# Transposing K from rows of 128 columns, and reading it with a step of two in the score matmuls

## The chip, the core and the metric

The kernel runs on one core of one Trainium2 chip. The time is that of the whole launch on that core, in device microseconds; the figure quoted for a kernel is the median of its runs. Inputs and outputs are bfloat16 in the chip's main memory (HBM). The core has a matrix engine (TensorE; PE in the profile, and PEld for its weight loads), three elementwise engines (VectorE, DVE; ScalarE, ACT; GpSimd, POOL), and a queue engine (SyncE, SP) that here only issues transfers. The transfers are carried out by the core's 16 DMA engines.

## The reference

Two attention blocks, A and B, of the same shape, with weights and caches of their own, are computed one after the other, and their results stand side by side in the output.

```
B, Sq, D = 16, 144, 448;  H, Sk, Dh = 16, 512, 256        # for A and for B
q      = (x @ wq), split into H heads                      # [B, H, Sq, Dh]
scores = einsum("bhqd,bhkd->bhqk", q, k_cache) * Dh**-0.5
p      = softmax(scores, axis=-1)
o      = einsum("bhqk,bhkd->bhqd", p, v_cache)
result = (o, heads joined) @ wo                            # [B, Sq, D]
out    = concatenate([result_A, result_B], axis=-1)
```

There are 2 x 16 x 16 = 512 pairs of batch and head. For each of them, K and V are 512 rows of 256 columns. The scores of one pair sum over the 256 columns of a head, which is more than the 128 rows of the matrix engine, so each score matmul is done in two halves of 128 columns that add up in the same accumulator.

## The kernel before

A "unit" is one pair of batch and head; eight units are a supergroup (64 of them), four are a group. The 144 queries of a unit are split into a part A of 112 queries and a part B of 32, so that four units' B parts fill the 128 output rows of the matrix engine. For each unit or group the work is:

- Q (function `t_q`, L314): eight matmuls of 128 rows by 144 columns make the transposed queries; VectorE or ScalarE scales them and copies them to `qt_sb` (L326, L330).
- SB (`t_sb`, L342): once for each supergroup, 16 matmuls make the part B scores of eight units. Four units share one output bank, each in its own 32 columns of the array (`tile_position=(0, 32 * j)`), so four matmuls can be in the array at a time. The stationary operand is 32 queries, the moving operand is a unit's 512 columns of transposed K.
- SA (`t_sa`, L418): for each unit, two matmuls (one for each half of the head) make the part A scores; the stationary operand is 112 queries, the moving operand 512 columns of transposed K.
- Softmax: VectorE takes the maximum (L354, L429), ScalarE the exponential and the row sum (L364, L440), VectorE the reciprocal (L374, L450), GpSimd multiplies (L382, L458).
- TA and TB (L471, L394): the matrix engine transposes the probabilities, 128 columns at a time. The columns are taken with a step of four elements from `pa_sb` and `pb_sb`; here the probabilities are the stationary operand and the identity is the moving one. VectorE copies the result out (L481, L403).
- PV (`t_pv`, L504): eight matmuls with V as the stationary operand; ScalarE copies the result into `ring` (L519).
- OP (`t_op_piece`, L542): the output projection, in pieces of two matmuls of 448 columns that are spread between the other work.

The order of each engine's instructions is written out by the program before the launch: a loop over slots `i` adds the steps of the units at fixed distances from each other (projection 15 slots ahead of PV, part A scores 5 ahead, part B scores 7 ahead), and a recording class works out which semaphores each step must wait for. Nothing is decided at run time; each engine runs its list in order.

K gets to the chip already transposed. `t_load_k` (L284 to L291) issues one transposing transfer for each supergroup on SP's queue: 4096 rows of 256 columns, which are 2 MB. The tile `kt_sb` has `NK` = 3 slots; in each of them lie, for each of the 128 partitions, first the 4096 elements of the head's first half (columns 0 to 127) and then the 4096 of its second half. Partition p holds columns p and 128 + p. V comes by plain transfers of 1 MB for each group (`t_load_v`, L299), also with three slots; x is transposed as K is (L280, L281); wq (L259, L261) and wo (L269) are plain transfers. All of these stand in one list on SP, sorted by the slot at which they are due. A transfer whose slot in SBUF is still being read makes SP wait, and everything behind it waits too.

Of the kernel before, what the change touches and what calls it, by code (L numbers as in the profile page):

```python
# [5 lines left out]
BF16 = mybir.dt.bfloat16  # L6
# [116 lines left out]
def bass_concat_heads__mha_block_cached__gqa_block_cached__near_ridge_kernel(  # L123
# [14 lines left out]
    ks = (A_k_cache, B_k_cache)  # L138
# [5 lines left out]
    H, SK, DH = A_k_cache.shape[1], A_k_cache.shape[2], A_k_cache.shape[3]  # L144
# [18 lines left out]
    NK, NV, NXG = 3, 3, 3  # L163
# [11 lines left out]
    with contextlib.ExitStack() as es:  # L175
        def sb(name, shape, dt):
            return es.enter_context(nc.sbuf_tensor(name, shape, dt))
# [4 lines left out]
        wq_sb = sb("wq_sb", [128, 4, H * DH], BF16)  # L182
        wo_sb = sb("wo_sb", [128, NWO, D], BF16)
        ring = sb("ring", [128, NWO, RC], BF16)
        kt_sb = sb("kt_sb", [128, NK, 2, 8 * SK], BF16)
        v_sb = sb("v_sb", [128, NV, 4, 4 * DH], BF16)
        xt_sb = sb("xt_sb", [128, NXG, 4, XB * SQ], BF16)
        qt_sb = sb("qt_sb", [128, NQT, 2, SQ], BF16)
# [29 lines left out]
        sems = {n: es.enter_context(nc.semaphore("s_" + n)) for n in sem_names}  # L218

        def unit(U):  # L220
            pr, r = divmod(U, NU)
            b, h = divmod(r, H)
            return pr, b, h
# [60 lines left out]
        def t_load_k(SG):  # L284
            pr, r0 = divmod(8 * SG, NU)
            sl = SG % NK
            src = ks[pr].rearrange("b h k d -> (b h k) d")[r0 * SK:(r0 + 8) * SK, :]

            def e(q):
                return q.dma_start_transpose(kt_sb[:, sl, :, :], src).then_inc(sems["kt%d" % sl], 16)  # L290
            S.add(SP, e, writes=[(("kt", sl), SG)], dma_sem="kt%d" % sl, name="k%d" % SG)  # L291

        def t_load_v(G):
# [39 lines left out]
        def t_sb(SG):  # L333
            ksl = SG % NK

            def e(t):
                ins = None
                for dc in range(2):
                    for jj in range(8):
                        U = 8 * SG + jj  # L340
                        j = jj % 4
                        ins = t.matmul(sb_ps[jj // 4][32 * j:32 * j + 32, :], lhsT=qt_sb[:, U % NQT, dc, QA:SQ],  # L342
                                       rhs=kt_sb[:, ksl, dc, jj * SK:(jj + 1) * SK], start=(dc == 0), stop=(dc == 1),
                                       tile_position=(0, 32 * j))
                return ins
            S.add(PE, e, reads=[(("qt", (8 * SG + jj) % NQT), 8 * SG + jj) for jj in range(8)] + [(("kt", ksl), SG)],
                  writes=[(("sbb", 0), ("s", 2 * SG)), (("sbb", 1), ("s", 2 * SG + 1))], banks=["sb0", "sb1"],
                  name="SB%d" % SG)
# [60 lines left out]
        def t_sa(U):  # L409
            SG = U // 8  # L410
            ksl = SG % NK
            bank = U % 2
            ko = (U % 8) * SK

            def e(t):
                ins = None
                for dc in range(2):
                    ins = t.matmul(sa_ps[bank][0:QA, :], lhsT=qt_sb[:, U % NQT, dc, 0:QA],  # L418
                                   rhs=kt_sb[:, ksl, dc, ko:ko + SK], start=(dc == 0), stop=(dc == 1))
                return ins  # L420
            S.add(PE, e, reads=[(("qt", U % NQT), U), (("kt", ksl), SG)], writes=[(("sap", bank), ("s", U))],
                  banks=["sa%d" % bank], name="SA%d" % U)
# [162 lines left out]
        for XG in range(NXGT):  # L585
            pr, j = divmod(XG, Bn // XB)
# [15 lines left out]
        for SG in range(NSG):  # L602
            dl = 8 * SG - LSB
            lo = 8 * (SG - NK) + 7 - LS + 1 if SG >= NK else s_min
            plan(lo, dl, 12, t_load_k, SG)
# [46 lines left out]
        while True:  # L652
# [51 lines left out]
            if 0 <= u < NT:  # L704
                t_pv(u)
                t_evac_ot(u)
                pr, b, h = unit(u)
# [19 lines left out]
            for bank in ("op", "qp"):  # L727
                while fifo[bank] and fifo[bank][0][2] <= i and credit >= 1 and (bank == "qp" or i >= op_hold):
# [3 lines left out]
                    pr = r // NCH  # L732
# [68 lines left out]
```

## Time and profile before

| | before |
|---|---|
| median of 3 runs | 1215.51 us (1214.79 to 1217.66) |
| profiled execution, first to last instruction (its span) | 1210.9 us |
| TensorE busy | 1176.6 us (97% of the span) |
| weight loads (beside the matmuls) | 902.6 us (75%) |
| VectorE, ScalarE, GpSimd busy | 770.1, 753.9, 679.6 us |
| mean granted TensorE clock | 0.997 |
| moved by the DMA engines | 294.15 MB, mean 243 GB/s |

The span runs from the first to the last instruction of the profiled execution. That execution has no time of its own outside the span on record; the median of the runs is 1215.51 - 1210.9 = 4.6 us longer than the span, which is what lies around it (start and end of the launch) as well as differences between executions. "Busy" is the time in which an engine had at least one instruction under way; matmuls overlap each other, so a busy matrix engine is not one at its peak. A line such as `L418 PE MATMUL sa_ps<-kt_sb,qt_sb 128*112 128x512 bf16 x1024` is a group: line 418 of the kernel, engine, operation, what is written from what is read, rows by columns of the stationary operand, shape of the moving one, and the number of instructions. `sa_ps` and the other names that end in `ps` are accumulators in PSUM.

### The profile page before, as it was taken

How to read it: one execution, taken by the hardware profiler on the slowest of the kernel's cores; microseconds unless marked ns; L12 is line 12 of the kernel's file. 1: busy time of each engine (PE TensorE's matmuls, PEld its weight loads, DVE VectorE, ACT ScalarE, POOL GpSimd, SP SyncE). 2: the span in 40 equal slices, each digit the busy share in tenths (PEclk: the TensorE clock that was granted, in tenths of full speed). 3: DMA queues.
4: the chain of work that ended last, by engine and by line, in shares of the span. 5: the costliest groups of instructions: out<-in, count | busy, mean ns of one | idle time of the engine just before them, and what ended most of it. 6: DMA issues, size and time to landing. Idle time of an engine off the chain costs nothing.

```text
span 1210.9 us, 33868 instructions
## 1 busy us (share of the span) xinstructions
PE 1176.6 (97%) x13952; PEld 902.6 (75%) x13952; DVE 770.1 (64%) x2179; ACT 753.9 (62%) x2213; POOL 679.6 (56%) x682
## 2 busy tenths in 40 slices
PE   4998999999999999999999999999999999999997
PEld 3676777777777777777777777777877777777765
DVE  1765666666666666666566666666666666666563
ACT  1655666666666666666566666666666666666553
POOL 0654565565555565565555655655655655655553
PEclk9999999999999999999999999999999999999999
DMA  9999999999999999999999999999999999999971
GB/s 250 296 269 290 246 255 225 242 251 246 245 238 234 228 263 231 239 239 233 278 284 272 278 272 267 247 257 224 245 245 236 226 245 244 244 239 243 223 178 47
DMA packets 627033, 294.15 MB, mean 243 GB/s; under 512 B 548416, under 2 KB 556608, under 8 KB 626880
## 3 DMA queue, kind: packets, MB, share of 16 engines
q1 hardware_dynamic: 625152, 287.85, 102.2%
q0 software_dynamic: 1728, 4.13, 1.2%
q8 instruction: 111, 1.82, 0.6%
q14 instruction: 42, 0.34, 0.1%
HBM read 148.90 MB, written 4.13 MB: 126 GB/s over the span
## 4 chain that ended last, share of the span: by engine, by line
PE 90%; DMA 6%; DVE 2%; SPq 1%; ACT 0%; issue 0%; POOL 0%; ACTq 0%
PE qp_ps L314 20%; PE ot_ps L504 19%; PE sa_ps L418 18%; PE op_ps L542 17%; PE sa_ps L471 8%; PE sb_ps L342 5%; DMA kt_sb<-in_A_k_cache_dram 4%; PE sb_ps L394 2%; DMA kt_sb<-in_B_k_cache_dram 1%; DVE stat L429 1%; DMA wq_sb<-in_A_wq_dram 0%; PE qp_ps L542 0%; SPq L280 0%; DVE qt_sb L326 0%; DVE pt_sb L481 0%
## 5 line engine op out<-in xcount | busy, mean ns | idle before, releaser
L458 POOL TENSOR_TENSOR pa_sb<-pa_sb,stat 112x512 bf16<-112x512 bf16 x512 | 532.7, 1041 | 491.6 <-DVE stat L450 491.4
L440 ACT ACTIVATE pa_sb<-sa_ps,stat 112x512 bf16<-112x512 f32 x512 | 352.0, 688 | 409.6 <-DVE stat L429 408.6
L429 DVE TENSOR_REDUCE stat<-sa_ps 112x1 f32<-112x512 f32 x512 | 353.9, 691 | 324.7 <-PE sa_ps L418 321.4
L314 PEld LDWEIGHTS qp_ps<-xt_sb,wq_sb 128*128 128x128 bf16 x4096 | 290.5, 99 | 93.1 <-issue 11.3
L314 PE MATMUL qp_ps<-xt_sb,wq_sb 128*128 128x144 bf16 x4096 | 344.1, 228 | 16.1 <-DMA wq_sb<-in_A_wq_dram 10.3
L504 PE MATMUL ot_ps<-pt_sb,v_sb 128*128 128x144 bf16 x4096 | 340.9, 226 | 0.0
L418 PE MATMUL sa_ps<-kt_sb,qt_sb 128*112 128x512 bf16 x1024 | 311.1, 385 | 1.0 <-DVE pt_sb L481 0.8
L542 PE MATMUL op_ps<-wo_sb,ring 128*128 128x448 bf16 x1120 | 279.6, 353 | 0.0
L504 PEld LDWEIGHTS ot_ps<-pt_sb,v_sb 128*128 128x128 bf16 x4096 | 269.1, 98 | 0.4
L471 PEld LDWEIGHTS sa_ps<-ident,pa_sb 112*128 112x128 bf16 x2048 | 161.2, 114 | 104.9 <-ACT pa_sb L440 24.8
L519 ACT ACTIVATE ring<-ot_ps 128x288 bf16<-128x288 f32 (+8 forms) x512 | 190.3, 372 | 4.5 <-PE ot_ps L504 4.5
L481 DVE COPY pt_sb<-sa_ps 128x448 bf16<-128x448 bf16 x512 | 190.5, 372 | 2.4 <-PE sa_ps L471 2.4
L471 PE MATMUL sa_ps<-ident,pa_sb 112*128 112x112 bf16 x2048 | 186.5, 213 | 0.1
L326 DVE TENSOR_SCALAR qt_sb<-qp_ps 128x288 bf16<-128x288 f32 x256 | 117.0, 457 | 98.2 <-PE qp_ps L314 97.5
L382 POOL TENSOR_TENSOR pb_sb<-pb_sb,stat 128x512 bf16<-128x512 bf16 x128 | 133.1, 1040 | 27.1 <-DVE stat L374 27.1
L330 ACT ACTIVATE qt_sb<-qp_ps 128x288 bf16<-128x288 f32 x256 | 106.0, 414 | 35.1 <-PE qp_ps L314 33.4
L418 PEld LDWEIGHTS sa_ps<-kt_sb,qt_sb 128*112 128x112 bf16 x1024 | 96.9, 129 | 38.5 <-issue 26.8
L542 PEld LDWEIGHTS op_ps<-wo_sb,ring 128*128 128x128 bf16 x1120 | 95.5, 98 | 28.1 <-issue 0.9
L440 ACT ACTIVATION_READ_ACCUMULATOR pa_sb<-sa_ps,stat 112x1 f32 x512 | 98.9, 193 | 0.0
L354 DVE TENSOR_REDUCE stat<-sb_ps 128x1 f32<-128x512 f32 x128 | 87.1, 680 | 3.6 <-PE sb_ps L342 3.6
L364 ACT ACTIVATE pb_sb<-sb_ps,stat 128x512 bf16<-128x512 f32 x128 | 88.5, 691 | 0.0
L450 DVE RECIPROCAL stat<-stat 112x1 f32<-112x1 f32 x512 | 78.4, 153 | 0.5 <-ACT pa_sb L440 0.5
(23 smaller groups left out, 368.4 us busy)
## 6 DMA issues: line engine op xcount, KB each, us to landing
v_sb<-in_A_v_cache_dram SPq DMA_DIRECT2D x64, 1024.0 KB, 6.0
v_sb<-in_B_v_cache_dram SPq DMA_DIRECT2D x64, 1024.0 KB, 6.1
out_dram<-ost_sb POOLq DMA_DIRECT2D x36, 112.0 KB, 5.1
wo_sb<-in_A_wo_dram SPq DMA_DIRECT2D x8, 448.0 KB, 7.4
wo_sb<-in_B_wo_dram SPq DMA_DIRECT2D x8, 448.0 KB, 5.7
wq_sb<-in_A_wq_dram SPq DMA_DIRECT2D x4, 768.0 KB, 6.2
wq_sb<-in_B_wq_dram SPq DMA_DIRECT2D x4, 768.0 KB, 7.8
wq_sb<-in_A_wq_dram SPq DMA_DIRECT2D x4, 128.0 KB, 6.6
```

Of the source, the lines that this page charges most:

```text
L314: ins = t.matmul(qp_ps[:, dc * SQ:(dc + 1) * SQ], lhsT=wq_sb[:, kc, c0:c0 + 128], rhs=xt_sb[:, xsl, kc, xo:xo + SQ], start=(kc == 0 and dc ...
L326: return v.tensor_scalar(qt_sb[:, sl, :, :], src, 1.0 / 16.0, None, op0=ALU.mult)
L382: return g.tensor_tensor(pb_sb[:, psl, :], pb_sb[:, psl, :], stat[:, RINVB + sl:RINVB + sl + 1].to_broadcast([128, SK]), op=ALU.mult)
L418: ins = t.matmul(sa_ps[bank][0:QA, :], lhsT=qt_sb[:, U % NQT, dc, 0:QA], rhs=kt_sb[:, ksl, dc, ko:ko + SK], start=(dc == 0), stop=(dc == 1))
L429: return v.tensor_reduce(stat[0:QA, NEG + sl:NEG + sl + 1], sa_ps[bank][0:QA, :], axis=AX.X, op=ALU.max, negate=True)
L440: return a.activation(pa_sb[0:QA, psl, :], sa_ps[bank][0:QA, :], AF.Exp, bias=stat[0:QA, NEG + sl:NEG + sl + 1], scale=1.0, accum_out=stat ...
L458: return g.tensor_tensor(pa_sb[0:QA, psl, :], pa_sb[0:QA, psl, :], stat[0:QA, RINV + sl:RINV + sl + 1].to_broadcast([QA, SK]), op=ALU.mult)
L471: ins = t.transpose(pta_ps[bank][:, c * 128:c * 128 + QA], src[:, c, :], ident[0:QA, 0:QA])
L481: return v.tensor_copy(pt_sb[:, sl, :, 0:QA], pta_ps[bank][:, 0:512].rearrange("p (c q) -> p c q", c=4)[:, :, 0:QA])
L504: ins = t.matmul(ot_ps[ob][:, dc * SQ:(dc + 1) * SQ], lhsT=v_sb[:, vsl, j, c * DH + dc * 128:c * DH + (dc + 1) * 128], rhs=pt_sb[:, sl, c, ...
L519: ins = a.activation(ring[:, 2 * h:2 * h + 2, c0:c0 + n1], src[:, :, 0:n1], AF.Copy)
L542: ins = t.matmul(acc[0:m, 0:D], lhsT=ring[:, c, col0:col0 + m], rhs=wo_sb[:, c, :], start=(c == first), stop=(c == last))
```

## The change

K is read as twice as many rows of half the length. A row of 256 columns is seen as two rows of 128, one after the other in memory: row 2k is the first half of key k, row 2k + 1 its second half. One transposing transfer takes 8192 such rows, 2 MB as before, and writes for each partition one run of 8192 elements. In `kt_sb` the two halves of a key now lie next to each other: element 2k belongs to the first half and element 2k + 1 to the second. So both kinds of score matmul (L342 and L418) take their 512 moving columns with a step of two elements, which is four bytes, from a stretch of 2048 bytes instead of 1024. The numbers of transfers, matmuls and waits, the order on all the engines, the sizes of the tiles and the results are the same.

```diff
-        kt_sb = sb("kt_sb", [128, NK, 2, 8 * SK], BF16)
+        kt_sb = sb("kt_sb", [128, NK, 8 * SK, 2], BF16)
...
         def t_load_k(SG):
             pr, r0 = divmod(8 * SG, NU)
             sl = SG % NK
-            src = ks[pr].rearrange("b h k d -> (b h k) d")[r0 * SK:(r0 + 8) * SK, :]
+            src = ks[pr].rearrange("b h k (c d) -> (b h k c) d", c=2)[r0 * SK * 2:(r0 + 8) * SK * 2, :]
 
             def e(q):
-                return q.dma_start_transpose(kt_sb[:, sl, :, :], src).then_inc(sems["kt%d" % sl], 16)
+                return q.dma_start_transpose(kt_sb[:, sl, :, :].rearrange("p k c -> p (k c)"), src).then_inc(sems["kt%d" % sl], 16)
...
                         ins = t.matmul(sb_ps[jj // 4][32 * j:32 * j + 32, :], lhsT=qt_sb[:, U % NQT, dc, QA:SQ],
-                                       rhs=kt_sb[:, ksl, dc, jj * SK:(jj + 1) * SK], start=(dc == 0), stop=(dc == 1),
+                                       rhs=kt_sb[:, ksl, jj * SK:(jj + 1) * SK, dc], start=(dc == 0), stop=(dc == 1),
                                        tile_position=(0, 32 * j))
...
                     ins = t.matmul(sa_ps[bank][0:QA, :], lhsT=qt_sb[:, U % NQT, dc, 0:QA],
-                                   rhs=kt_sb[:, ksl, dc, ko:ko + SK], start=(dc == 0), stop=(dc == 1))
+                                   rhs=kt_sb[:, ksl, ko:ko + SK, dc], start=(dc == 0), stop=(dc == 1))
```

## The prediction

> **What bounds the kernel now.** I read the share of busy time first, then the busy time by stages, the waits of the matrix engine, the groups by shape, and last the transfers. The page's first part and the stages:
>
> ```profile
> PE 1176.6 (97%) x13952; PEld 902.6 (75%) x13952; DVE 770.1 (64%) x2179; ACT 753.9 (62%) x2213; POOL 679.6 (56%) x682
> ```
> ```profile
> 24.00:60.00 36.00, 32.91 (x390) 23.08 (x382) 23.85 (x67) 21.77 (x62) 19.15 (x19) 1.00 1.16 291
> 60.00:120.00 60.00, 54.03 (x647) 41.13 (x647) 36.01 (x102) 34.69 (x99) 32.03 (x33) 1.00 1.17 280
> 120.00:360.00 240.00, 239.74 (x2878) 183.66 (x2877) 160.17 (x455) 155.87 (x466) 141.46 (x141) 1.00 1.05 243
> ```
>
> The columns after the length are the busy time of PE, PEld, DVE, ACT and POOL, then the granted clock, the DMA share and GB/s. From 120 us on TensorE has work in 239.74 of 240 us at full clock: it is the bound, and what a matmul costs goes straight into the time. Only before 120 us does it stand still noticeably. What for, with the starts of the six matmul groups that waited for K (idle time and its end in brackets):
>
> ```profile
> PE qp_ps L314 <- DMA wq_sb<-in_A_wq_dram: 10.3, 1, 10.3
> PE sb_ps L342 <- DMA kt_sb<-in_A_k_cache_dram: 7.9, 4, 2.3
> PE sb_ps L342 <- DMA kt_sb<-in_B_k_cache_dram: 0.8, 2, 0.4
> ```
> ```profile
> 72.96 0.40 PE L342 MATMUL sb_ps<-kt_sb,qt_sb 128*32 128x512 bf16 x4 [2.28 <-DMA kt_sb<-in_A_k_cache_dram]
> 94.12 0.40 PE L342 MATMUL sb_ps<-kt_sb,qt_sb 128*32 128x512 bf16 x4 [1.55 <-DMA kt_sb<-in_A_k_cache_dram]
> 112.75 0.40 PE L342 MATMUL sb_ps<-kt_sb,qt_sb 128*32 128x512 bf16 x4 [2.14 <-DMA kt_sb<-in_A_k_cache_dram]
> 585.46 0.40 PE L342 MATMUL sb_ps<-kt_sb,qt_sb 128*32 128x512 bf16 x4 [1.96 <-DMA kt_sb<-in_A_k_cache_dram]
> ```
>
> So all that K's transfers cost the end is 7.9 + 0.8 = 8.7 us. The reader should also see "x4 ... 0.40": four matmuls of 512 columns end 0.40 us after the first began, where one takes 0.379. Four run side by side, and count once. The groups that carry the rest:
>
> ```profile
> L418 PE MATMUL sa_ps<-kt_sb,qt_sb 128*112 128x512 bf16 x1024 | 311.1, 385 | 1.0 <-DVE pt_sb L481 0.8
> L504 PE MATMUL ot_ps<-pt_sb,v_sb 128*128 128x144 bf16 x4096 | 340.9, 226 | 0.0
> L314 PEld LDWEIGHTS qp_ps<-xt_sb,wq_sb 128*128 128x128 bf16 x4096 | 290.5, 99 | 93.1 <-issue 11.3 <-ACT qt_sb L330 4.9 <-DVE qt_sb L326 4.6
> L418 PEld LDWEIGHTS sa_ps<-kt_sb,qt_sb 128*112 128x112 bf16 x1024 | 96.9, 129 | 38.5 <-issue 26.8 <-DVE pt_sb L481 1.9
> L394 PEld LDWEIGHTS sb_ps<-ident,pb_sb 128*128 128x128 bf16 x512 | 35.6, 114 | 0.2
> L342 PEld LDWEIGHTS sb_ps<-kt_sb,qt_sb 128*32 128x32 bf16 x1024 | 21.9, 96 | 33.5 <-issue 10.4 <-DVE pt_sb L403 3.8 <-ACT qt_sb L330 0.8
> ```
>
> And K's transfers, by line of issue, with the matmuls of the same tile:
>
> ```profile
> L342 PE MATMUL sb_ps<-kt_sb,qt_sb x1024: 376/379/634, 23.7 to 1170.5; 128*32 128x512 bf16 x171
> L418 PE MATMUL sa_ps<-kt_sb,qt_sb x1024: 379/379/583, 28.9 to 1194.5; 128*112 128x512 bf16 x171
> L290 SPq DMA_TRANSPOSE kt_sb<-in_A_k_cache_dram x32: 8081/11996/15442, 8.0 to 570.0; - x32
> L290 SPq DMA_TRANSPOSE kt_sb<-in_B_k_cache_dram x32: 9066/12276/16996, 585.7 to 1151.8; - x32
> ...
> DMA to landing us min/median/max: 10.8/15.0/20.5
> ```
>
> **The stepped read: 2048 matmuls, all on the bound.** Median durations are 379 ns for 512 columns and 226 for 144 (L504's mean): (379 - 226) / 368 = 0.416 ns a column, so 512 columns stream in 213 ns; the other 166 overlap with the next matmul. Part A has 1024 matmuls one after the other. Part B has 1024 in 256 sets of four. If a step of two slowed the stream by d per 512 columns, the end would move by (1024 + 256) x d = 1280 d. No matmul of before has a stepped moving operand, so d has to be bounded. Below nothing it can't be, since contiguous matmuls of 144, 448 (352 ns) and 512 columns all stream at 0.41 to 0.42 ns a column. For the upper end there is one stepped read on this engine: the transposes' weight loads take every fourth element of 128. They take 114 ns, against 99 for 128 contiguous ones. With 32 contiguous columns at 96 ns and 112 at 129, an ordinary load costs 33 / 80 = 0.41 ns a column over a fixed 83 ns. Then the contiguous load of 128 streams in 16 ns, some four columns at a time, and the stepped one in 31 ns: twice as long. Doubling the matmul's 213 ns gives d = 213 and 1280 x 0.213 = 273 us. Read as a flat 15 ns for each instruction, it gives 19 us. I take d = 0. The stepped load still delivers a column every 31 / 128 = 0.24 ns, with a step twice as large as the change's; the matmul asks for one every 0.416 ns. The ordinary load of 112, at 0.41 ns a column, is its nearest relative, and the doubled one is the kind that runs four abreast. Both ends stay for the range.
>
> The row shows a step of four at twice the contiguous load time. The Trainium skill (SBUF — State Buffer, the note on cachelines under Door 1) says that SBUF has lines of 16 bytes and that two hits on each are enough for full speed. By it a step of four bf16 (two hits) is free as well as a step of two (four hits): it makes d = 0, as I take it, but doesn't explain the 15 ns, so I do not lean on it.
>
> **K's transfer: the same bytes in the same number of 256-byte pieces, read from neighbouring addresses.** The page counts 548416 packets under 512 B, and K's 64 x 8192 half rows of 256 B are 524288 of them; the change keeps that number unless the engines join neighbours. One load in a window of 12 us (206 to 218, in 40 slices) shows its pace:
>
> ```profile
> GB/s 310 228 125 267 342 211 20 1 9 9 97 291 290 289 290 291 290 289 290 291 290 289 290 291 290 289 290 291 290 289 458 196 96 158 253 371 396 389 410 403
> ```
>
> It is flat at 290 GB/s with a gap, which looks like a fixed price for each packet: 2.10 MB / 290 = 7.2 us of the 15.0 us from issue to landing. Bounds come from the landings: all loads as the fastest (10.8) is 4.2 us less each, all as the slowest (20.5) is 5.5 more. Faster can only take the waits away: at most 8.7 us. Slower is covered at first: a load issued at 201.83 lands at the median near 216.8 and is read at 220.96, 4.1 us later. Beyond that cover, 5.5 - 4.1 = 1.4 us per supergroup x 64 = 90 us, plus a few at the six places that have no cover. I take 0. The nearest rows are the two transposes of x, both of rows 896 B apart: 1728 pieces take SP about 3.44 us and 576 about 1.69 to 2.01, or 1.2 to 1.5 ns a further piece, and K's 8192 in 12.0 us are 1.46 ns each. The shape with one column block and the shape with several cost alike; neighbouring rows none of them shows.
>
> For transposing transfers the Trainium skill (DMA: Bandwidth & Descriptors, Latency and other measured facts) gives 261 GB/s where the rows are not contiguous and some 350 to 400 where they are. This speaks for a gain: by estimate 2.10 MB in 5.2 to 6.0 us, 1.2 to 2.0 us less per load, which would shorten the waits by 5.6 to 8.3 us, to about 1207 to 1210. The flat 290 here lies between its two figures.
>
> **What moves.** The instruction order, the waits and the semaphores are the same on all five engines. On SP, V's transfers (L299) stand behind K's; they wait for their slots to be read, 235.3 us for L542 alone, so an earlier end of K's issue only lengthens that wait, and a later one is covered by it. Weight loads of L418 and L342 read the unchanged `qt_sb`: nothing.
>
> **Sum.** 1210.9 us of span + 0 (read) + 0 (transfer) = 1210.9; with the 4.6 us to the median, 1215.5, written as 1215. One measurement of this kernel spreads by about 0.24% over three runs, so I call 0.3% (3.6 us) no change.
>
> **The rivals.**
> - *Faster K loads.* Neighbouring pieces are read faster; the waits at 73, 94, 113 and 585 us shrink. For it: three lie in the stretch with the DMA share at 1.17. Against: the pace is flat, as a price per packet is. At most 8.7 us: 1206.8; a gain of over 3.6 us needs over 40% of the waits.
> - *A small price of the step* (other side). d of 3 to 15 ns, by the weight-load row read as flat: +3.8 to +19 us, 1219 to 1235. It decides from d = 2.9 ns.
> - *The step halves the stream* (other side). Against: the stepped load's 0.24 ns a column. Both parts: +273 less the K waits of 8.7, some 1480. If only the four matmuls side by side suffer: 256 x 0.213 = 55, about 1270.
> [...]
> - That the change doesn't do what it says is excluded: the one transfer has the same bytes and the matmuls read the tile it writes.
>
> **How the numbers follow.** No effect 0.32 (1212 to 1219); faster loads 0.28 (1207 to 1212); small price 0.19 (1219 to 1235); halved stream 0.16 (1270 to 1480); slower loads 0.05 (1219 to 1305). The likeliest is no effect: 1215. The range from 1206 to 1236 leaves out the halved stream and most of the slower loads, 0.2. Faster 0.28, same 0.32, slower 0.16 + 0.19 + 0.05 = 0.40.
>
> **What would show it.** Right: L418 and L342 stay at 379 ns, pairs of L418 start 0.21 us apart, K lands near 15 us, and the six waits stay. A small price shows as 380 to 395 ns there and nowhere else; a halved stream as 590; faster loads as fewer packets or a plateau over 290 GB/s with the waits gone. I am wrong if the matrix engine can't take stepped columns at its full pace; that is the largest risk.

## The result, and the profile after

The changed kernel takes 1225.76 us (median of 4 runs, 1224.3 to 1226.28); the kernel before, measured beside it, takes 1215.15 us (1214.35 to 1217.66). The ratio is 1.0088, with a 95% interval of 1.0072 to 1.0104: 0.9% slower, clear of the 0.3% that the prediction called no change. The profiled execution of the changed kernel took 1225.71 us with a span of 1224.0 us, so 1.7 us lie outside the span; the 4.6 us that the prediction added for this were partly a difference between executions.

The same parts of the page and the same waits as shown for the kernel before, now of the changed kernel (busy time and share of each engine; then what the matrix engine waited for: microseconds in total, times, longest):

```profile
PE 1190.6 (97%) x13952; PEld 904.0 (74%) x13952; DVE 774.4 (63%) x2179; ACT 753.8 (62%) x2213; POOL 679.9 (56%) x682
```
```profile
PE qp_ps L314 <- DMA wq_sb<-in_A_wq_dram: 10.2, 1, 10.2
PE sb_ps L342 <- DMA kt_sb<-in_A_k_cache_dram: 6.5, 5, 1.9
...
PE sb_ps L342 <- DMA kt_sb<-in_B_k_cache_dram: 2.0, 1, 2.0
```

TensorE is busy 14.0 us longer (1190.6 against 1176.6), and the span is 13.1 us longer. It waits for K 8.5 us in all, against 8.7. So the time did not come from a wait; it is matrix work. Which work, the groups by shape tell (busy time and mean duration behind the bar):

```profile
L314 PE MATMUL qp_ps<-xt_sb,wq_sb 128*128 128x144 bf16 x4096 | 344.4, 228 | 15.9 <-DMA wq_sb<-in_A_wq_dram 10.2 <-DVE qt_sb L326 3.1 <-ACT qt_sb L330 2.6
L504 PE MATMUL ot_ps<-pt_sb,v_sb 128*128 128x144 bf16 x4096 | 341.0, 226 | 0.0
L418 PE MATMUL sa_ps<-kt_sb,qt_sb 128*112 128x512 bf16 x1024 | 322.1, 395 | 1.0 <-DVE pt_sb L481 0.8
L542 PE MATMUL op_ps<-wo_sb,ring 128*128 128x448 bf16 x1120 | 279.0, 353 | 0.0
L342 PE MATMUL sb_ps<-kt_sb,qt_sb 128*32 128x512 bf16 x1024 | 71.4, 397 | 9.8 <-DMA kt_sb<-in_A_k_cache_dram 6.5 <-DMA kt_sb<-in_B_k_cache_dram 2.0 <-issue 0.6
```

The part B group of the kernel before:

```profile
L342 PE MATMUL sb_ps<-kt_sb,qt_sb 128*32 128x512 bf16 x1024 | 67.9, 385 | 10.5 <-DMA kt_sb<-in_A_k_cache_dram 7.9 <-DMA kt_sb<-in_B_k_cache_dram 0.8 <-issue 0.6
```

L314, L504 and L542 stand within 0.6 us of where they stood (344.1, 340.9 and 279.6 us before). L418 has 322.1 us instead of 311.1, and L342 has 71.4 instead of 67.9: these two groups carry it. The tile of K in the changed kernel (durations in ns: shortest, median, longest):

```profile
L342 PE MATMUL sb_ps<-kt_sb,qt_sb x1024: 385/388/632, 23.8 to 1183.3; 128*32 128x512 bf16 x171
L418 PE MATMUL sa_ps<-kt_sb,qt_sb x1024: 385/388/672, 29.4 to 1207.6; 128*112 128x512 bf16 x171
L290 SPq DMA_TRANSPOSE kt_sb<-in_A_k_cache_dram x32: 8377/12114/15751, 7.4 to 577.5; - x32
L290 SPq DMA_TRANSPOSE kt_sb<-in_B_k_cache_dram x32: 9282/11832/16351, 591.5 to 1164.4; - x32
...
DMA to landing us min/median/max: 12.1/15.0/19.7
```

Both kinds of score matmul went from a median of 379 ns to 388, and the shortest of L418 went from 379 to 385, so it is all of them and not a few. K's transfers kept their 12 us of issue and 15.0 us to landing. What counts for the bound is how soon the next matmul can start. The same moment of a supergroup in the two kernels shows it, first before, then after (start in us; length of the merged group, which is a row of instructions of one line taken together):

```profile
218.85 0.64 PE L418 MATMUL sa_ps<-kt_sb,qt_sb 128*112 128x512 bf16 x2
219.33 0.36 PE L471 MATMUL sa_ps<-ident,pa_sb 112*128 112x112 bf16 x4
```
```profile
221.19 0.66 PE L418 MATMUL sa_ps<-kt_sb,qt_sb 128*112 128x512 bf16 x2
221.69 0.36 PE L471 MATMUL sa_ps<-ident,pa_sb 112*128 112x112 bf16 x4
```

The transposes begin 0.48 us after the pair of score matmuls before, and 0.50 us after it now. From the start times of all instructions in the two traces, the median from the start of an L418 matmul to the next start is 216 ns before and 227 after. The 16 part B matmuls of a supergroup, from the first one's start to the start of what follows them, took a median of 977 ns and now take 1026, which is 12 ns more for each of the four sets. The pace of the whole kernel follows: from the part B matmuls of supergroup 6 to those of supergroup 60, where nothing waits for K but in a few places in the middle, before and after:

```profile
132.29 0.40 PE L342 MATMUL sb_ps<-kt_sb,qt_sb 128*32 128x512 bf16 x4
1114.81 0.40 PE L342 MATMUL sb_ps<-kt_sb,qt_sb 128*32 128x512 bf16 x4
```
```profile
133.59 0.41 PE L342 MATMUL sb_ps<-kt_sb,qt_sb 128*32 128x512 bf16 x4
1126.96 0.41 PE L342 MATMUL sb_ps<-kt_sb,qt_sb 128*32 128x512 bf16 x4
```

These are 982.5 and 993.4 us for 54 supergroups: 0.20 us more for each, and 0.20 x 64 = 12.9 us over the kernel. Part A has 16 matmuls in a supergroup and part B four sets of four, so 20 x 11 ns = 0.22 us were to be expected.

### The profile page after: what moved, and what is told of

Same layout as the page of the kernel before. It is cut to its first block, busy times and chain, and to the rows that moved or that the text cites. A ratio compares the mean times of both kernels' runs of the same rounds, so it can differ in the third digit from the quotient of the medians.

```text
span 1224.0 us, 33868 instructions
## 1 busy us (share of the span) xinstructions
PE 1190.6 (97%) x13952; PEld 904.0 (74%) x13952; DVE 774.4 (63%) x2179; ACT 753.8 (62%) x2213; POOL 679.9 (56%) x682
## 2 busy tenths in 40 slices
DMA packets 627033, 294.15 MB, mean 240 GB/s; under 512 B 548416, under 2 KB 556608, under 8 KB 626880
## 4 chain that ended last, share of the span: by engine, by line
PE 90%; DMA 6%; DVE 2%; SPq 1%; issue 0%; ACT 0%; POOL 0%; ACTq 0%
PE sa_ps L418 19%; PE ot_ps L504 19%; PE qp_ps L314 19%; PE op_ps L542 17%; PE sa_ps L471 8%; PE sb_ps L342 5%; DMA kt_sb<-in_A_k_cache_dram 4%; PE sb_ps L394 2%; DMA kt_sb<-in_B_k_cache_dram 2%; DVE stat L429 1%; DVE pt_sb L481 0%; PE qp_ps L542 0%; DVE pt_sb L403 0%; SPq L259 0%; SPq L299 0%
## 5 line engine op out<-in xcount | busy, mean ns | idle before, releaser
L314 PE MATMUL qp_ps<-xt_sb,wq_sb 128*128 128x144 bf16 x4096 | 344.4, 228 | 15.9 <-DMA wq_sb<-in_A_wq_dram 10.2
L314 PEld LDWEIGHTS qp_ps<-xt_sb,wq_sb 128*128 128x128 bf16 x4096 | 290.9, 99 | 92.9 <-issue 11.2
L504 PE MATMUL ot_ps<-pt_sb,v_sb 128*128 128x144 bf16 x4096 | 341.0, 226 | 0.0
L418 PE MATMUL sa_ps<-kt_sb,qt_sb 128*112 128x512 bf16 x1024 | 322.1, 395 | 1.0 <-DVE pt_sb L481 0.8
L542 PE MATMUL op_ps<-wo_sb,ring 128*128 128x448 bf16 x1120 | 279.0, 353 | 0.0
L504 PEld LDWEIGHTS ot_ps<-pt_sb,v_sb 128*128 128x128 bf16 x4096 | 269.3, 98 | 0.4
L471 PEld LDWEIGHTS sa_ps<-ident,pa_sb 112*128 112x128 bf16 x2048 | 162.2, 114 | 114.6 <-ACT pa_sb L440 24.7
L471 PE MATMUL sa_ps<-ident,pa_sb 112*128 112x112 bf16 x2048 | 185.3, 212 | 0.1
L418 PEld LDWEIGHTS sa_ps<-kt_sb,qt_sb 128*112 128x112 bf16 x1024 | 97.1, 129 | 40.4 <-issue 28.7
L542 PEld LDWEIGHTS op_ps<-wo_sb,ring 128*128 128x128 bf16 x1120 | 95.2, 98 | 27.6 <-ACT ring L519 0.2
L342 PE MATMUL sb_ps<-kt_sb,qt_sb 128*32 128x512 bf16 x1024 | 71.4, 397 | 9.8 <-DMA kt_sb<-in_A_k_cache_dram 6.5
```

Of the source, the lines that this page charges most:

```text
L314: ins = t.matmul(qp_ps[:, dc * SQ:(dc + 1) * SQ], lhsT=wq_sb[:, kc, c0:c0 + 128], rhs=xt_sb[:, xsl, kc, xo:xo + SQ], start=(kc == 0 and dc ...
L471: ins = t.transpose(pta_ps[bank][:, c * 128:c * 128 + QA], src[:, c, :], ident[0:QA, 0:QA])
L504: ins = t.matmul(ot_ps[ob][:, dc * SQ:(dc + 1) * SQ], lhsT=v_sb[:, vsl, j, c * DH + dc * 128:c * DH + (dc + 1) * 128], rhs=pt_sb[:, sl, c, ...
L542: ins = t.matmul(acc[0:m, 0:D], lhsT=ring[:, c, col0:col0 + m], rhs=wo_sb[:, c, :], start=(c == first), stop=(c == last))
```

## The experiments

Is it the read or the transfer? The first two kernels do one half of the change each.

**The transfer alone.**

```diff
 (the changed kernel, with)
-  rhs=kt_sb[:, ksl, ko:ko + SK, dc]
+  rhs=kt_sb[:, ksl, :, :].rearrange("p k c -> p (k c)")[:, 2 * ko + dc * SK:2 * ko + (dc + 1) * SK]
...
```

> Only the transfer is changed: K is transposed from rows of 128 columns as in the changed kernel, but the score matmuls take 512 columns in a row from the interleaved tile, so the scores mix the two halves of the keys (the computation is changed, the work isn't). Theory READ (the step of two costs about 11 ns in each 512-column matmul, 1280 of them on the path): 1215 us, L418 and L342 back at 379 ns. Theory LOAD (the price comes from the transfer or from its order in the tile): 1226 us.

Measured: 1213.75 us, ratio 0.9999 (0.9985 to 1.0012) to the kernel before. Its tile of K:

```profile
L418 PE MATMUL sa_ps<-kt_sb,qt_sb x1024: 379/379/676, 30.8 to 1195.2; 128*112 128x512 bf16 x171
...
DMA to landing us min/median/max: 10.9/15.1/20.4
```

The transfer from neighbouring rows neither costs nor gains anything that the interval lets one see (1.8 us either way), and the order of the data in the tile does no harm by itself.

**The read alone.**

```diff
 (the kernel before, with)
-  rhs=kt_sb[:, ksl, dc, ko:ko + SK]
+  rhs=kt_sb[:, ksl, :, :].rearrange("p c k -> p (c k)").rearrange("p (k s) -> p k s", s=2)[:, ko:ko + SK, dc]
...
```

> Only the read is changed: K is transposed as in the kernel before (two blocks), and the score matmuls take their columns with a step of two out of that tile, which mixes keys in the scores. READ: 1226 us, L418 and L342 at 388 ns. LOAD: 1215 us and 379 ns.

Measured: 1224.72 us, ratio 1.0088 (1.0064 to 1.0113), with both groups at 388 to 389 ns. This is the change's whole loss (1.0088 too), within the interval. What remains is why a step of two costs 11 ns.

**A step of four**, with `s=4` in the place of `s=2` and the unit's number modulo 4 as the offset.

> As the read alone, with a step of four elements (8 bytes; keys are mixed in the scores, and some are read twice). Theory REACH (the stream is held by the bytes that the columns span: 1024 B are free, 2048 B take 224 ns instead of 213, a pace of 9.1 B per ns): 4096 B take 448 ns, 235 ns more in 1280 matmuls, about 1515 us, matmuls of some 610 ns. Theory FLAT (any step costs the same start-up of 11 ns for a matmul): 1226 us and 388 ns. Theory NEIGHBOURS (columns that are not fetched in adjacent pairs cost 11 ns in all, however far apart): 1226 us.

Measured: 1500.26 us (one execution).

```profile
L418 PE MATMUL sa_ps<-kt_sb,qt_sb x1024: 610/633/642, 28.9 to 1481.9; 128*112 128x512 bf16 x171
```

REACH had said 1515 us and 610 ns, where the median is 633; FLAT and NEIGHBOURS had said 1226, and fall. From start to start the median is 453 ns, against REACH's 448: 433 where the second half of the same unit follows, 455 where the transposes (L471) do.

**Adjacent pairs with gaps of two.**

```diff
 (the kernel before, with)
-  rhs=kt_sb[:, ksl, dc, ko:ko + SK]
+  rhs=kt_sb[:, ksl, :, :].rearrange("p c k -> p (c k)").rearrange("p (k s t) -> p k s t", s=2, t=2)[:, (U % 8) * 256:(U % 8 + 1) * 256, dc, :]
...
```

> As the read alone, but the columns are taken in adjacent pairs with a gap of two behind each (512 columns out of the same 2048 bytes as with a step of two; keys are mixed in the scores). REACH: 1226 us and 388 ns, since the bytes spanned are the same. FLAT: 1226 us if a pattern of two dimensions counts as a step. NEIGHBOURS: 1215 us and 379 ns.

Measured: 1224.33 us (one execution), medians of 388 and 389 ns, 228 ns from start to start: as with single elements at a step of two. Whether neighbours are taken in pairs makes no difference.

REACH leaves two readings: the bytes from the first column to the last, or the stretches of 16 bytes that are touched. The second is suggested by the size of a line that the Trainium skill gives for this memory (SBUF — State Buffer, Specifications). The next two kernels tell them apart.

**Runs of eight with gaps of eight**, the same pattern with `t=8` and 64 runs for a matmul.

> As the read alone, but the columns are taken in runs of eight (16 bytes) with a gap of eight behind each, so they span 2048 bytes as with a step of two, and lie in every second stretch of 16 bytes only (keys are mixed in the scores). Theory SPAN (the bytes from the first to the last column count): 1225 us, L418 and L342 at 388 ns. Theory LINES (the stretches of 16 bytes that are touched count, about 1.75 to 1.79 ns each; 512 columns in a row touch 64, in runs of eight with gaps 64, with a step of two 128, with a step of four 256): 1215 us and 379 ns.

Measured: 1214.43 us, ratio 0.9991 (0.9978 to 1.0005).

```profile
L418 PE MATMUL sa_ps<-kt_sb,qt_sb x1024: 379/379/521, 29.6 to 1195.5; 128*112 128x512 bf16 x171
```

The 512 columns span 2048 bytes as with a step of two, with gaps, and cost nothing. SPAN falls.

**A step of sixteen**, `s=16`, where every column has a stretch of 16 bytes for itself.

> Step of sixteen elements (32 bytes; keys are mixed in the scores and read more than once): each of the 512 columns lies in a stretch of 16 bytes of its own, with an unused one between. LINES: 512 x 1.79 = 916 ns of stream, 703 more than before, x 1280 = 900 us, about 2110 us. SPAN: 16384 bytes at 9.1 B per ns are 1800 ns, 1587 more, about 3240 us.

Measured: 2094.01 us (one execution), within 1% of LINES' 2110 and far from 3240.

```profile
L418 PE MATMUL sa_ps<-kt_sb,qt_sb x1024: 1076/1099/1145, 30.2 to 2075.2; 128*112 128x512 bf16 x171
```

**The step of two on matmuls of 144 columns.**

```diff
 (the kernel before, with)
-  rhs=xt_sb[:, xsl, kc, xo:xo + SQ]
+  rhs=xt_sb[:, xsl, kc - kc % 2:kc - kc % 2 + 2, :].rearrange("p c k -> p (c k)").rearrange("p (k s) -> p k s", s=2)[:, xo:xo + SQ, kc % 2]
```

> K and the score matmuls are as before; here the 4096 projection matmuls of 144 columns (L314) take their moving columns with a step of two (queries and parts of the sum are mixed up). LINES: 288 bytes lie in 18 or 19 stretches before and 36 or 37 with the step, 37 x 1.79 = 66 ns against 60 for the columns alone and 63 between the starts before; about 3 ns x 4096 = 12 us more, 1227 us. FLAT (11 ns per matmul): 45 us more, 1260 us. If the 63 ns come from the weight loads alone and cover the read: 1215 us.

Measured: 1220.24 us, ratio 1.0044 (1.0031 to 1.0057), so 5.3 us more, less than half of LINES' 12. FLAT's 45 us is out again, and so is a full cover by the weight loads. The starts of these matmuls lie 65 ns apart instead of 63; LINES asked for 66. Two ns x 4096 are 8 us. By the kernel's offsets, which are multiples of 576 bytes, a matmul touches 36 stretches and not 37 if the tile begins at a multiple of 16 bytes; 36 x 1.79 = 64.4 ns would be some 6 us. The size of this term is met only roughly, and a change of 2 ns is a weak test.

**The step in part A alone**, with L342 as before.

> The read alone, with the step in L418 only; L342 reads in a row as before (keys are mixed in part A's scores). If the 1024 matmuls of part A carry 11 ns each and the 256 sets of part B the rest: 11.3 us more than before, 1226, against 14 for both. If the four matmuls side by side pay the larger part: at most 5 us more, 1220 us.

Measured: 1222.16 us, ratio 1.0074 (1.0049 to 1.0100), or 9.0 us (6.0 to 12.2) more. Both parts together had 10.7 (7.8 to 13.7). Part A carries most of it. The split for part B, 2.8 us by 256 x 11 ns, is within the intervals and not resolved by them. The traces resolve it: the 16 part B matmuls of a supergroup take 977 ns in this kernel as before, and 1026 with the read alone and in the changed kernel, with four still side by side (`x4 ... 0.41`).

Put together, the medians from start to start in the traces:

```
512 columns of L418              16-byte stretches   start to start   per stretch
in a row                          64                 216 ns           (column pace)
runs of eight, gaps of eight      64                 216              (column pace)
step of two; pairs               128                 227; 228         1.77; 1.78 ns
step of four                     256                 453              1.77
step of sixteen                  512                 918              1.79
```

These fit a simple rule: a matmul takes the longer of two times, 0.416 ns for each column, and some 1.8 ns for each stretch of 16 bytes. Stretches of another size do not fit. By stretches of 32 bytes the runs of eight would cost what the step of two costs (64 of them each), and by stretches of 8 the step of sixteen would cost what the step of four costs (512 each). The price per stretch is not one exact number: with a step of four it is 1.69 ns where the second half follows and 1.78 where the transposes do, with a step of sixteen 1.75 (898 ns) and 1.79 (919); why is open. By 1.79, the stretches would begin to decide for 512 columns (213 ns) at 213 / 1.79 = 119 of them. That point is an estimate from the rule, since no kernel here touches between 64 and 128 stretches. A step of two in bf16 touches 128, just beyond it, so the small price of 11 ns hangs on the exact value: at 1.69 ns the 128 stretches would take 216 ns, as long as 512 columns in a row.

## Why the prediction was right or wrong

*The stepped read: the step that failed.* The prediction put d between 0 and 213 ns, and took d = 0 because the stepped weight load delivers a column every 0.24 ns where the matmul asks for one every 0.416. The runs give d = 11. The mechanism that was priced (a slower stream in 1280 matmuls on the bound) is the right one, and 1280 x 0.011 = 14.1 us is close to the 14.0 us of added busy time and the 13.1 of span. The 10.6 us between the medians (8.7 to 12.6 by the interval) are less; where the rest went, no run shows. The measured 1225.76 us lies inside the stated range of 1206 to 1236 because the range kept the small price as a rival; the sum did not have it. The term was mis-sized by treating "delivers a column" as one pace: the stream has a price for each stretch of memory beside that for each column. The row that the prediction leaned on can be read that way. The stepped weight load's 31 ns, if its 128 columns come as four parts of 32 in 16 stretches each at the same time, are 1.9 ns a stretch, near the 1.79 of the matmuls. No run here took that load apart, so this is argued and not shown.

*The two ends.* The flat reading of the weight-load row, 15 ns for each instruction and 19 us, came nearer than either the value taken or the doubling, but for another reason: the step of four shows that the price is not flat, and that doubling the stream is what a step of four does (453 against 216).

*The rule on cachelines.* The prediction reported from the Trainium skill (SBUF — State Buffer, the note under Door 1) that two hits on a line of 16 bytes are enough for full speed, and did not lean on it. Here four hits (a step of two) cost 11 ns in 216, and two hits (a step of four) double the time (453), at a granted clock of 0.997 to 0.999 in these profiles; eight hits cost nothing. The measurement decides: for the moving operand of these matmuls two are not enough. By the rule above about 4.3 (512 / 119) would be, which is an estimate.

*The transfer.* Right: 0 was taken, the transfer alone has the ratio 0.9999, and K lands at 15.0 us as before. A load in the changed kernel, in a window of 12 us from 208.2 (40 slices):

```profile
GB/s 269 238 150 143 274 327 166 6 3 9 9 151 289 290 289 292 289 290 289 292 289 290 289 292 289 290 289 292 289 290 289 438 247 14 151 109 289 355 355 410
DMA packets 8523, 2.89 MB, mean 241 GB/s; under 512 B 8165, under 2 KB 8165, under 8 KB 8521
```

It is the same flat 290 GB/s, in packets of the same size. The page of the changed kernel counts 548416 packets under 512 B, as before, so the pieces are not joined. The 350 to 400 GB/s of the Trainium skill (DMA: Bandwidth & Descriptors, Latency and other measured facts) for contiguous transposes did not appear, and with it went the rival of faster loads. Slower loads did not come either: the times to landing span 12.1 to 19.7 us, 10.8 to 20.5 before.

*Order and waits.* Right in the sum: no instruction changed its place in the order, and K's waits are 8.5 us instead of 8.7, again at six places. Those of supergroups 3, 4 and 5 recur (1.31, 1.36 and 1.88 us instead of 2.28, 1.55 and 2.14) and that of supergroup 32 too (2.01 instead of 0.42); the other two moved, from supergroups 31 and 33 to 0 and 2.

*The rivals.* The small price of the step, given 3 to 15 ns, 1219 to 1235 us and a chance of 0.19, is what happened: 380 to 395 ns had been named as its sign, and 388 were measured. The prediction gave more to each of two other cases, no effect and faster loads. That the three slower cases together had 0.40, more than either, should have been a warning: the forecast named the single likeliest case while the side that was likeliest was the other one.

## What to carry to other kernels

A layout that makes a transfer simpler moves its price to whoever reads it: when the reader is the bound, a few ns in every instruction decide, and a transfer that is already hidden gives nothing back. Before a matmul is given a stepped moving operand, count the 16-byte stretches it touches, times some 1.8 ns, and compare with 0.416 ns times its columns; here, in bf16, runs of eight that fill a stretch were free at the one gap tried (eight), a step of two cost 5% of the stream, and a step of four doubled it. And when no instruction of the kind to be priced is in the trace, a short range of possible prices times the number of instructions on the bound is worth more than the most plausible single price: 1280 x 3 ns was already enough to be seen.

## What the runs showed of the hardware that was not expected

- The moving operand of a matmul is held by 16-byte stretches at 1.77 to 1.79 ns each by the medians as well as by columns at 0.416 ns; the rule fits at 128, 256 and 512 stretches (227, 453, 918 ns), and for 144 columns within 1 ns (65 measured, 64 to 66 worked out).
- Four matmuls side by side, each with its own moving operand, pay this together and not one after the other: sets of four take 0.41 us instead of 0.40 with the step of two, 12 ns more in the pace of a set against 11 for a single matmul.
- Transposing K out of rows that lie next to each other runs at the same 290 GB/s as out of rows 512 bytes apart (one load of each kernel), and lands at the same median of 15.0 us.
